# Decay attention and two MLPs on one core: the last tile's scores of two heads by one block-diagonal matrix of queries, and a new order

## The chip, the cores and the metric

The kernel runs on one core of a Trainium2 chip. The metric is device microseconds of one execution. Five engines run side by side, each through its own instructions in a fixed order: TensorE (PE in the profile, with its weight loads as PEld), VectorE (DVE), ScalarE (ACT), GpSimd (POOL) and the queue that issues the transfers (SP). They wait for each other on semaphores.

## The reference, cut to what matters

```python
# q, k, v: (4 batches, 8 heads, 576 positions, 64 dims); f: (4, 8, 576)
scores = q @ k.T / 8
cum = np.cumsum(np.log(np.clip(f, 0.0001, 1.0)), axis=-1)
scores = np.where(causal, -1e9, scores + cum[..., :, None] - cum[..., None, :])
scores = scores - scores.max(-1, keepdims=True)
attn = np.exp(scores)
attn = attn / (attn.sum(-1, keepdims=True) + 1e-9)
x = (attn @ v)                      # reshaped to (2304 tokens, 512)
x = relu(x @ moe_w_in) ** 2 @ moe_w_out          # 512 -> 2048 -> 512
g = x @ moe2_w_gate                              # 512 -> 1536
out = (silu(g) * (x @ moe2_w_val)) @ moe2_w_out  # 1536 -> 512
```

All inputs and the output are float32.

## The kernel before, in words

**Precision.** TensorE multiplies float16 or rounded float32. A float32 operand is split into a high and a low part and three products (high by high, high by low, low by high) are added up in PSUM. The passes (0,0), (0,1), (1,0) in the code are these three.

**Attention.** A unit is one batch and two heads: 16 units. Both heads' queries and keys lie in one tile, dims by positions, head 0 on partitions 0 to 63 and head 1 on 64 to 127, so a product over one head's 64 dims uses half of the array's rows. Query positions are cut in tiles of 128. The first 256 (two tiles) of all units are the early half, the positions 256 to 575 the late half: two tiles of 128 queries and a last tile of 64, called the tail, which the late half takes first. For the tail the 576 keys are cut in two pieces of 288 (`cuts`), and the code makes one step of six products for each piece: three passes by two heads, each of 64 contraction rows (line 802, `scores`). Head 0 has 64 columns of queries. Head 1 takes 128 columns (the last 128 queries), so that its 64 wanted rows come out on PSUM partitions 64 to 127; the other 64 rows are not read. Each head has its own PSUM tile.

After the scores: VectorE adds the decay and finds the minimum (line 825), ScalarE takes the exponential (845) and the high part of the probabilities (904), VectorE the low part (908), a DMA transposes them, TensorE multiplies by the values (955, `mix`), ScalarE and VectorE keep the result as `x` (978, 983). On the way in, ScalarE rounds keys and queries (742, 735), GpSimd takes their low parts (745, 738) and masks the decay table (786).

**MLPs.** Tiles of 256 tokens. The first MLP's first product is line 1151 into `h`; ScalarE applies relu, square and the cast (1173, 1180, 1194), GpSimd the low part (1199), and line 1221 is its second product into `acc`, which ScalarE and VectorE empty at the end of a tile (1240, 1242). The second MLP is lines 1417 and 1533. Weights arrive as float32, are looked through for a scale (407, 324, 333) and split in two float16 parts on ScalarE and VectorE (378, 381, 386, 466, 470).

**The order.** Nothing is scheduled at run time. `Plan` collects steps with an engine, an assumed duration, what they depend on and which buffers they take; its `order()` walks through them once and gives each engine, when it is free, the ready step with the lowest number in `pri`. The tables `EPRI`, `VPRI`, `IPRI`, `ILOAD`, `OPRI`, `OLOAD` and `GPRI` hold such numbers for the early attention units and for the loading of weights; `FREE` says how many of the four pieces of the first weight matrix load without waiting for the first decay table. The result is a written-out list for each engine, which the engines run through in that order, whether or not the assumed durations were right.

**Fillers.** `keep_clock` (line 293) is a product of ones into a spare PSUM bank, 130 times, of the lowest priority: the plan puts one where TensorE would have nothing and a bank of `h` is free. All 130 stand in TensorE's list and are carried out, wherever they came to stand.

Of the kernel before, what the change touches and what calls it, by code (L numbers as in the profile page):

```python
# [9 lines left out]
F32R = mybir.dt.float32r  # L10
# [4 lines left out]
AF = mybir.ActivationFunctionType  # L15
# [3 lines left out]
PE, ACT, DVE, POOL, SP = "PE", "ACT", "DVE", "POOL", "SP"  # L19
AFTER = {PE: 0.25, ACT: 0.2, DVE: 0.15, POOL: 0.2, SP: 0.0, None: 0.0}  # L20
DMA_ISSUE = 0.45
QUEUE = 8
PORT = {DVE: 1.0, POOL: 0.45}
GLO = 9
SUMV = 3
# [31 lines left out]
class Plan:  # L57
# [104 lines left out]
    return 0.1 + n * 0.0021  # L162


GPRI = 863
GATE0 = -1
GATE = 5
EPRI = [97, 98, -1473, -437, 74, 58, -88, -342, 192, 243, 591, 593, 223, 341, 56, -118]
VPRI = [79, -116, 547, 595]
IPRI, ILOAD = [573, -458, 265, 171], [-574, -104, -303, 434]  # L170
OPRI, OLOAD = [157, 400, 363, 178], [-547, 34, 61, 213]
VERBOSE = False
WHOLE = 2
SQUARE = 7
FREE = 4
COPY = (ACT, ACT)
ROUNDS = [(0, 1), (8,), (2, 3), (4, 5), (6, 7)]
LAST = ROUNDS[-1]
# [3 lines left out]
def decay_attention_moe_kernel(ctx: ExitStack, tc, q, k, v, f, w1, w2, wg, wv, wo, outT):  # L182
    nc = tc.nc
    P = 128
    B, H, _, S = q.shape
# [7 lines left out]
    TAIL = S // P  # L193
    NB = TAIL + 1
    SPLIT = 256
    QW = S - SPLIT
# [6 lines left out]
    AN, ACC = 4, 2  # L203
# [16 lines left out]
    ps_at = attn_ctx.enter_context(tc.tile_pool(name="ps_at", bufs=AN, space=bass.MemoryType.PSUM))  # L220
    pools = {}
# [7 lines left out]
    add = plan.add  # L229
# [13 lines left out]
    one = table("one", 1)  # L243
# [13 lines left out]
    def prev(tag):  # L257
        return alloc_chain.get(tag)
# [296 lines left out]
    XFIRST, XSTAT = {}, {}  # L555
# [117 lines left out]

            XSTAT["x8"] = add(DVE, 0.7, widest, [XSTAT[x] for x in range(B)], pri)

    SCALED, BIAS = {}, {}

    def attn_unit(idx, b, pr, half, opened):
        early = half == 0
        whole = early and b < WHOLE  # L680
        pri = EPRI[idx] if early else 10 * idx
# [6 lines left out]
        q0 = 0 if early else SPLIT  # L688
# [4 lines left out]
        c = {}  # L693
# [55 lines left out]
        KA, QA = (kr, qr) if early else (kq_buf("KA"), kq_buf("Q"))  # L749
# [15 lines left out]
        VT = vu["buf"]  # L765
        seen = {0: [], 1: []}
        for ti, i in enumerate(tiles):
# [24 lines left out]
            mm = None  # L792
            for ci, (n0, n1) in enumerate(cuts):

                def scores(heads=heads, n0=n0, n1=n1, ti=ti, ci=ci):
                    for h in range(2):
                        c["ps", ti, ci, h] = at_tile()
                    for qi, ki in ((0, 0),) if early else ((0, 0), (0, 1), (1, 0)):
                        for h, _, _, qc, M, _ in heads:
                            rows = slice(64 * h, 64 * h + 64)  # L800
                            Q, K = (c["qr"], c["kr"]) if early else (c["Q"][:, qi], c["K"][:, ki])
                            nc.tensor.matmul(  # L802
                                c["ps", ti, ci, h][:M, : n1 - n0], Q[rows, qc - q0 : qc - q0 + M],
                                K[rows, n0:n1], start=(qi, ki) == (0, 0), stop=early or qi == 1,
                            )

                bufs = [*sbufs, cg_buf] if ci == 0 else []
                pbufs = [Buf("ps_at", AN) for _ in range(2)]
                mm = add(PE, (4 if early else 3) * (0.06 + (n1 - n0) * 0.00048), scores, [*ready, opened], pri,
                         take=[*pbufs, *bufs], order=[mm, *(prev(x.tag) for x in bufs)])  # L810
# [128 lines left out]
            def mix(st=st, i=i, nb=nb, w=w, ti=ti):  # L939
                c["av", ti] = ps = at_tile()  # L940
                for blk in range(nb if whole else 0):
                    for h in range(2):
                        nc.tensor.matmul(
                            ps[64 * h : 64 * h + 64, :w], vu["vr"][:, blk, 64 * h : 64 * h + 64], st["PT"][:, h, blk, :],
                            start=blk == 0, stop=blk == nb - 1,
                        )
                for blk in range(nb if not whole else 0):
                    K = min(P, S - blk * P)
                    for a, va in ((0, 0), (0, 1), (1, 0)):
                        for h in range(2):  # L950
                            if i == TAIL:
                                rhs = st["PT"][:K, 0, a, blk, 64 * h : 64 * h + 64]
                            else:
                                rhs = st["PT"][:K, h, a, blk, :]
                            nc.tensor.matmul(  # L955
                                ps[64 * h : 64 * h + 64, :w], vu["VT"][:K, blk, h, va, :], rhs,
                                start=(blk == 0 and (a, va) == (0, 0)), stop=(blk == nb - 1 and a == 1),
                            )

            o = P * i - q0  # L960
# [4 lines left out]
            mx = add(PE, 0.05 + nb * 0.3 if whole else 0.2 + nb * 6 * 0.03, mix, [tn, *vu["in"], XSTAT[xk], opened], pri,  # L965
                     take=[pbuf])
            t_buf.users.append(mx)
            VT.users.append(mx)

            kx = XS[:, b : b + 1] if whole else kx_of(xk, b, pr)  # L970
# [634 lines left out]
    def open_half():  # L1605
        h0_ctx.close()
        pools["at"] = attn_ctx.enter_context(
            tc.tile_pool(name="at", bufs=1, side="right", reuse_waits="tile")
        )

    opened = fence(open_half, half0_ops)
    for b in range(B):
# [116 lines left out]
```

## Time and profile before

| | us |
|---|---|
| median of 3 runs (lowest, highest) | 956.33 (955.98, 957.39) |
| the profiled execution's own time | 958.73 |
| its span, first to last instruction | 957.0 |
| TensorE busy with products | 945.6 |
| VectorE busy | 621.3 |
| ScalarE busy | 603.4 |
| GpSimd busy | 315.2 |

Busy times are unions: two products of which one starts before the other ends count once. The duration of one product is from its start to its modelled end and includes the way through the array, so products that follow each other closely overlap; what a product adds to the time is the distance from its start to the next one's start.

### The profile page before, as it was taken

To read this page: it belongs to the slowest core of one execution; us is meant where nothing else is said; L and a number is where in the kernel's file an instruction comes from. 1 tells how busy PE (TensorE), PEld (TensorE's weight loads), DVE (VectorE), ACT (ScalarE), POOL (GpSimd) and SP (SyncE) were. 2 spreads that over 40 slices of the span, in tenths; PEclk is the share of its full clock that TensorE was granted. 3 is DMA by queue.
4 is the path that set the end of the run, shared out by engine and by line. 5 is a ranking of instruction groups with operands and counts; after the bars stand their busy time and mean duration, and the time that the engine had idled before them with its cause. 6 is when DMAs were issued, how large, how long until landed. Compare 5 with 4: busy or idle time off the path is not lost.

```text
span 957.0 us, 22589 instructions
## 1 busy us (share of the span) xinstructions
PE 945.6 (99%) x8941; PEld 735.7 (77%) x8941; DVE 621.3 (65%) x1438; ACT 603.4 (63%) x1145; POOL 315.2 (33%) x422
## 2 busy tenths in 40 slices
PE   8999999999999999999999999999999999999998
PEld 4578777887777877778888887778977776877774
DVE  5689878576766788787989897445464363433331
ACT  5899898697788897777978675235343343332332
POOL 1332054354444353443335453031311241111120
PEclk9999999999999999999999999999999999999999
DMA  8796339687968799999934411002020001000101
GB/s 285 231 340 215 97 78 225 187 212 143 192 147 186 183 229 182 252 242 243 206 110 177 155 48 42 1 2 89 2 67 1 1 2 45 2 1 12 34 1 45
DMA packets 147946, 117.48 MB, mean 123 GB/s; under 512 B 98240, under 2 KB 136128, under 8 KB 142592
## 3 DMA queue, kind: packets, MB, share of 16 engines
q1 hardware_dynamic: 147840, 116.04, 46.7%
q8 instruction: 70, 1.15, 0.5%
q14 instruction: 36, 0.29, 0.1%
HBM read 83.44 MB, written 9.51 MB: 97 GB/s over the span
## 4 chain that ended last, share of the span: by engine, by line
PE 54%; DVE 1%; ACT 0%; issue 0%; DMA 0%; SPq 0%; DVEq 0%; ACTq 0%
PE v L1417 15%; PE acc L1533 14%; PE h L1417 11%; PE acc L1221 7%; PE h L1151 6%; PE ps L955 1%; PE ps L802 1%; DVE ms L1287 0%; DVE p L908 0%; DVE s L825 0%; DMA out_dram<-tmp 0%; DVE sq L1291 0%; SPq L1591 0%; DVE VT L630 0%; DVE tmp L1564 0%
## 5 line engine op out<-in xcount | busy, mean ns | idle before, releaser
L1151 PE MATMUL h<-x,i 128*128 128x256 f16 x1728 | 208.4, 273 | 0.7 <-ACT hold L1173 0.7
L1221 PE MATMUL acc<-g,o 128*128 128x256 f16 x1728 | 208.0, 273 | 0.0
L1151 PEld LDWEIGHTS <-i 128*128 128x128 f16 x1728 | 163.0, 98 | 29.3 <-issue 8.4
L1221 PEld LDWEIGHTS <-o 128*128 128x128 f16 x1728 | 163.8, 98 | 27.4 <-issue 6.0
L1533 PE MATMUL acc<-o,f 128*128 128x512 f16 (+1 forms) x720 | 145.9, 358 | 0.9 <-ACT o L1506 0.5
L1533 PEld LDWEIGHTS <-f 128*128 128x128 f16 x720 | 70.0, 98 | 65.0 <-issue 1.4
L1199 POOL TENSOR_TENSOR g<-tmp,g 128x512 f16<-128x512 f32 x56 | 76.1, 1360 | 130.7 <-ACT g L1194 126.0
L1496 POOL TENSOR_TENSOR tmp<-tmp,o 128x256 f32<-128x256 f32 (+1 forms) x30 | 23.5, 784 | 247.7 <-ACT o L1490 247.3
L786 POOL TENSOR_SCALAR_AFFINE_SELECT bias<-bias 128x128 f32<-128x128 f32 (+1 forms) x160 | 60.9, 390 | 106.3 <-DVE cg L825 58.3
L908 DVE SCALAR_TENSOR_TENSOR p<-s,cg,p 128x512 f16<-128x512 f32 (+4 forms) x112 | 76.0, 695 | 24.9 <-ACT p L904 24.4
L845 ACT ACTIVATE s<-s,cg 128x256 f32<-128x256 f32 (+4 forms) x144 | 83.0, 578 | 13.8 <-DVE cg L825 13.5
L825 DVE CUSTOM_DVE_ANT_0 s<-ps,bias 128x512 f32<-128x512 f32 (+3 forms) x160 | 72.6, 481 | 29.4 <-PE ps L802 21.4
L904 ACT ACTIVATE p<-s,cg 128x512 f16<-128x512 f32 (+4 forms) x112 | 67.1, 615 | 9.5 <-DVE cg L858 4.6
L1462 ACT ACTIVATE r<-r,ms 128x768 f32<-128x768 f32 (+1 forms) x30 | 26.1, 871 | 74.1 <-DVE r L1434 74.0
L1417 PEld LDWEIGHTS <-g 128*128 128x128 f16 x720 | 65.4, 98 | 8.5 <-issue 0.6
L1417 PEld LDWEIGHTS <-v 128*128 128x128 f16 x720 | 65.4, 98 | 6.5
L1417 PE MATMUL v<-i,g 128*128 128x256 f16 (+1 forms) x540 | 67.9, 262 | 0.2 <-DVE tmp L1434 0.2
L1417 PE MATMUL v<-i,v 128*128 128x256 f16 (+1 forms) x540 | 67.9, 262 | 0.0
L1434 DVE TENSOR_TENSOR r<-r,h 128x512 f32<-128x512 f32 (+1 forms) x30 | 19.0, 633 | 73.7 <-PE h L1417 65.1
L1434 DVE TENSOR_TENSOR r<-r,v 128x512 f32<-128x512 f32 (+1 forms) x60 | 38.1, 634 | 33.8 <-PE v L1417 31.7
L1500 POOL TENSOR_TENSOR r<-r,o 128x768 f32<-128x768 f32 (+1 forms) x30 | 45.4, 1513 | 39.6 <-ACT o L1493 38.7
L1417 PEld LDWEIGHTS <-eg 128*128 128x128 f16 x540 | 49.3, 98 | 8.9
(186 smaller groups left out, 1604.2 us busy)
## 6 DMA issues: line engine op xcount, KB each, us to landing
raw<-in_moe_w_out_dram SPq DMA_DIRECT2D x11, 1024.0 KB, 6.5
bias<-cum_d SPq DMA_DIRECT2D x16, 576.0 KB, 4.8
raw<-in_moe_w_val_dram SPq DMA_DIRECT2D x9, 1024.0 KB, 5.7
raw<-in_moe_w_gate_dram SPq DMA_DIRECT2D x9, 1024.0 KB, 6.7
raw<-in_moe_w_in_dram SPq DMA_DIRECT2D x8, 1024.0 KB, 7.1
vr<-in_v_dram SPq DMA_DIRECT2D x32, 256.0 KB, 4.2
x_d<-tmp SPq DMA_DIRECT2D x18, 256.0 KB, 2.7
kr<-in_k_dram SPq DMA_DIRECT2D x16, 288.0 KB, 4.2
```

What stands on the lines that cost most here:

```text
L786: nc.gpsimd.affine_select(diag, diag, pattern=[[-1, w]], compare_op=ALU.is_ge, fill=-8e9, base=0, channel_multiplier=1)
L825: nc.vector.tensor_tensor_reduce(out=s[r0:r1, n0:e1], in0=c["ps", ti, ci, h][r0:r1, : e1 - n0], in1=c["bias"][r0:r1, h, n0:e1], scale=-0.1 ...
L845: nc.scalar.activation(s[:, :ext], s[:, :ext], AF.Exp, bias=cg[:, mc : mc + 1], scale=-1.0, accum_out=cg[:, 2:3],)
L904: nc.scalar.activation(pv[:, 0, :ext], s[:, :ext], AF.Copy, scale=cg[:, 3:4])
L908: nc.vector.scalar_tensor_tensor(pv[:, 1, :ext], s[:, :ext], cg[:, 3:4], pv[:, 0, :ext], op0=ALU.mult, op1=ALU.subtract,)
L1151: nc.tensor.matmul(HP[key][:, u, :], w[:, wi, kk, c * P : (c + 1) * P], x[:, xi, kk, :], start=(kk == 0 and (wi, xi) == (0, 0)), stop=(kk ...
L1199: lows[2].tensor_tensor(G[k0][1][:, 1], G[k0][0], G[k0][1][:, 0], op=ALU.subtract)
L1221: nc.tensor.matmul(acc[:, d - part[0], :], w[:, wi, c, d * P : (d + 1) * P], G[k0][1][:, gi, u, :], start=(m == 0 and d == part[0] and (wi ...
L1417: nc.tensor.matmul(R[reg][:, which, :w], t[:, wh, w1_ : w1_ + P], x[:, xh, xi, kk], start=fresh and which == 0 and kk == 0 and (wh, xh) == ...
L1434: nc.vector.tensor_tensor(out(), x(), y(), op=ALU.add)
L1500: nc.gpsimd.tensor_tensor(g, g, R["g"][:, 0, 1:4], op=ALU.subtract)
L1533: nc.tensor.matmul(acc_of(d), wd[:, cc, d * P : (d + 1) * P], R["g"][:, gi, 2 * m : 2 * m + 2].rearrange("p a t -> p (a t)"), start=mm == ...
```

## The change: what it does

The tail's two heads now share their products. A new tile `both` (two buffers, taken in turn by even and odd units) holds for the high and for the low part of the queries a matrix of 128 by 128: head 0's 64 tail queries in the upper left quarter, head 1's in the lower right, zeros elsewhere. The zeros are written once, by two ScalarE instructions where the late half opens; two GpSimd copies for each unit bring in the queries. With this matrix as the stationary operand one product over all 128 rows gives head 0's scores on PSUM partitions 0 to 63 and head 1's on 64 to 127 of one bank. So a unit's tail needs six products (three passes by two pieces of keys) of 128 rows, 128 columns and 288 keys, in place of twelve of 64 rows, and they stand in one step, both pieces together, in place of two steps. VectorE's and all later instructions keep their forms.

Beside that: the numbers of the priority tables and `FREE` (4 to 2) are others, the plan's assumed durations for late scores and for `mix` are others, and `mix` is rewritten for groups of tiles, which `MERGE = (0, 0)` leaves switched off (one tile a group, as before).

```diff
+TAIL_US = 0.95
+MERGE = (0, 0)
-GPRI = 863
+GPRI = 842
-EPRI = [97, 98, -1473, -437, 74, 58, -88, -342, 192, 243, 591, 593, 223, 341, 56, -118]
+EPRI = [370, 281, -956, -100, 16, 121, -583, -685, 358, 313, 446, 543, -150, 12, -61, -51]
...
-FREE = 4
+FREE = 2
...
+            both = Buf("both%d" % (idx % 2), 1)
+            def corner(h):
+                def copy():
+                    r = slice(64 * h, 64 * h + 64)
+                    nc.gpsimd.tensor_copy(BOTH[idx % 2][r, :, r], c["Q"][r, :, QW - 64 : QW])
+                return copy
+            b0 = take(POOL, 0.3, corner(0), [qh, ql], [both], use=[QA])
+            b1 = add(POOL, 0.3, corner(1), [qh, ql], pri, use=[QA, both], order=[b0])
+            tail_ready = [kh, kl, b0, b1]
...
-                heads = [(0, 0, 64, S - 64, 64, 0), (1, 64, 128, S - 128, 128, 0)]
+                heads = [(0, 0, 64, S - 64, 64, 0), (1, 64, 128, S - 64, 64, 0)]
...
+                def tail_scores(cuts=cuts, ti=ti):
+                    for cc, (m0, m1) in enumerate(cuts):
+                        c["ps", ti, cc, 0] = c["ps", ti, cc, 1] = at_tile()
+                        for qi, ki in ((0, 0), (0, 1), (1, 0)):
+                            nc.tensor.matmul(
+                                c["ps", ti, cc, 0][:, : m1 - m0], BOTH[idx % 2][:, qi], c["K"][:, ki, m0:m1],
+                                start=(qi, ki) == (0, 0), stop=qi == 1,
+                            )
...
+                if i == TAIL:
+                    if ci == 0:
+                        tbufs = [Buf("ps_at", AN) for _ in cuts]
+                        mm = add(PE, TAIL_US, tail_scores, [*tail_ready, opened], pri, take=[*tbufs, *bufs],
+                                 use=[both], order=[prev(x.tag) for x in bufs])
+                    pbufs = [tbufs[ci]] * 2
...
+        for n in range(2):
+            BOTH[n] = pools["at"].tile([P, 2, P], F32R, tag=f"both{n}", name="both")
+            nc.scalar.activation(
+                BOTH[n].rearrange("p a q -> p (a q)"), one[:, 0:1].to_broadcast([P, 2 * P]), AF.Copy, scale=0.0
+            )
```

In the changed kernel the lines have other numbers: 293 is 295, 1151 is 1193, 1221 is 1263, 955 is 995, 802 is 817 and, for the tail, 826; GpSimd's 738 is 740, 786 is 801, and the copies are 767.

What this makes of the order, first on TensorE at the first tail. `KA` is the keys, `Q` and `both` the queries, `i` and `o` weights of the first MLP. Before:

```order
L1221 MATMUL acc<-g,o_1320 128x256
L802 MATMUL ps<-KA,Q 64x288
L802 MATMUL ps<-KA,Q 128x288
L802 MATMUL ps<-KA,Q 64x288
L802 MATMUL ps<-KA,Q 128x288
L802 MATMUL ps<-KA,Q 64x288
```

and so on to twelve. Now:

```order
L1193 LDWEIGHTS i_614
L1193 MATMUL h<-x,i_614 128x256
L826 MATMUL ps<-KA,both 128x288 x6
L817 MATMUL ps<-KA,Q 128x512 x6
L1193 LDWEIGHTS i_614
```

The twelve half-row products are six of 128 rows. Over the whole list there were 29 visits to line 802 for tails (26 of six products and 3 of twelve) and are 16 visits to line 826 of six.

Second, on TensorE, the fillers around the first product of line 1221. Before, 15 of them stand there, the last of the 130:

```order
L1151 LDWEIGHTS i_1374
L1151 MATMUL h<-x,i_1374 128x256
L293 LDWEIGHTS ones
L293 MATMUL ps<-ones 128x512
L293 LDWEIGHTS ones
L293 MATMUL ps<-ones 128x512
```

Now one stands there:

```order
L1193 LDWEIGHTS i_1302
L1193 MATMUL h<-x,i_1302 128x256
L295 LDWEIGHTS ones
L295 MATMUL ps<-ones 128x512
L1263 LDWEIGHTS o_1219
L1263 MATMUL acc<-g,o_1219 128x256
```

and 19 stand late in the attention, around the tail of a unit near the end:

```order
L295 LDWEIGHTS ones
L295 MATMUL ps<-ones 128x512
L817 MATMUL ps<-KA,Q 128x384 x6
L826 MATMUL ps<-KA,both 128x288 x6
L295 LDWEIGHTS ones
L295 MATMUL ps<-ones 128x512
```

Ahead of the first product of line 1221 there were 130 fillers and are 109; two more come after the 19.

Third, on GpSimd, where the third late unit's queries are split. Before:

```order
L745 TENSOR_TENSOR KA<-kr,KA 128x576
L738 TENSOR_TENSOR Q<-qr,Q 128x320
L921 MEMSET p_3489 128x2x64
L1199 TENSOR_TENSOR g<-tmp,g 128x512
L786 AFFINE_SELECT bias<-bias 128x128 x2
```

Now:

```order
L747 TENSOR_TENSOR KA<-kr,KA 128x576
L801 AFFINE_SELECT bias<-bias 128x128
L740 TENSOR_TENSOR Q<-qr,Q 128x320
L801 AFFINE_SELECT bias<-bias 128x128
L767 COPY both<-Q 64x2x64 x2
L1241 TENSOR_TENSOR g<-tmp,g 128x512
```

The two copies of the unit stand behind the low part of its queries and ahead of a low part of the MLP.

## Rows read from the trace of the kernel before

**Rows 1.** The page: busy time by engine.
```profile
PE 945.6 (99%) x8941; PEld 735.7 (77%) x8941; DVE 621.3 (65%) x1438; ACT 603.4 (63%) x1145; POOL 315.2 (33%) x422
```

**Rows 2.** The chain that ended last, by engine.
```profile
PE 54%; DVE 1%; ACT 0%; issue 0%; DMA 0%; SPq 0%; DVEq 0%; ACTq 0%
```

**Rows 3.** Waits of PE, 0 to 480 us: us in total, times, longest.
```profile
PE ps L407 <- DVE raw L386: 1.1, 2, 0.6
PE ps L802 <- DVE cg L825: 0.9, 1, 0.9
```

**Rows 4.** Timeline of PE: start, length, products (three parts of it).
```profile
185.55 2.13 PE L1221 MATMUL acc<-g,o 128*128 128x256 f16 x18
187.61 1.06 PE L802 MATMUL ps<-KA,Q 64*64 64x288 f32 x12
...
188.60 1.49 PE L1151 MATMUL h<-x,i 128*128 128x256 f16 x12
...
198.94 0.83 PE L1221 MATMUL acc<-g,o 128*128 128x256 f16 x6
199.70 0.66 PE L802 MATMUL ps<-KA,Q 64*64 64x288 f32 x6
200.29 0.83 PE L1221 MATMUL acc<-g,o 128*128 128x256 f16 x6
```

**Rows 5.** Groups by line and form: busy, mean ns, idle before.
```profile
L802 PE MATMUL ps<-KA,Q 64*128 64x288 f32 x96 | 20.1, 320 | 0.0
...
L879 PEld LDWEIGHTS ps<-p,s 128*128 128x128 f32 x96 | 11.5, 191 | 1.3 <-issue 1.0
```

**Rows 6.** Timeline of PE at line 879, float32 over all 128 rows.
```profile
49.62 1.69 PE L293 MATMUL ps<-ones 128*128 128x512 bf16 x7
51.15 1.50 PE L879 MATMUL ps<-p,s 128*128 128x128 f32 x12
```

**Rows 7.** Timeline of PE at the first product of line 1221.
```profile
117.92 3.83 PE L293 MATMUL ps<-ones 128*128 128x512 bf16 x15
121.60 1.67 PE L1221 MATMUL acc<-g,o 128*128 128x256 f16 x13
```

**Rows 8.** Stretches: us, busy of PE, PEld, DVE, ACT, POOL, clock, DMA share, GB/s.
```profile
60.00:147.00 87.00, 86.23 (x790) 69.62 (x788) 74.65 (x220) 79.65 (x167) 27.08 (x50) 1.00 0.53 155
147.00:190.00 43.00, 42.96 (x453) 34.55 (x449) 29.73 (x98) 33.10 (x82) 16.99 (x27) 1.00 0.85 203
190.00:300.00 110.00, 110.00 (x1269) 87.90 (x1268) 75.13 (x202) 89.12 (x184) 51.45 (x84) 1.00 0.80 175
...
400.00:480.00 80.00, 79.62 (x945) 63.40 (x944) 66.00 (x171) 63.58 (x125) 29.97 (x44) 1.00 0.98 229
```

**Rows 9.** Waits of ACT, 60 to 150 us.
```profile
ACT hold L1173 <- PE h L1151: 4.2, 8, 1.9
ACT g L1194 <- PE acc L1221: 1.9, 3, 1.1
```

**Rows 10.** Timeline of ACT, what two products of line 1221 wait for.
```profile
119.84 1.12 ACT L1194 CAST g<-hold 128x512 f16<-128x512 f32 x2
...
146.24 0.67 ACT L1240 ACTIVATE tmp<-acc,fy 128x512 f32<-128x512 f32 x1
```

**Rows 11.** Timeline of PE at the second of these.
```profile
147.34 0.82 PE L1221 MATMUL acc<-g,o 128*128 128x256 f16 x6
```

**Rows 12.** Groups of POOL by form: busy, mean ns, idle before.
```profile
L738 POOL TENSOR_TENSOR Q<-qr,Q 128x320 fp32r<-128x320 f32 x16 | 14.6, 912 | 2.9 <-ACT Q L735 2.9
...
L786 POOL TENSOR_SCALAR_AFFINE_SELECT bias<-bias 64x64 f32<-64x64 f32 x32 | 10.0, 312 | 6.7 <-DMA bias<-cum_d 5.5
...
L635 POOL MEMSET vr<- 64x128 f32 x32 | 6.1, 202 | 19.3 <-PE ps L943 7.2 <-issue 6.2 <-DVE cg L855 2.6
```

**Rows 13.** Timeline of POOL, low part of the first late unit's queries.
```profile
185.56 0.87 POOL L738 TENSOR_TENSOR Q<-qr,Q 128x320 fp32r<-128x320 f32 x1
```

**Rows 14.** Groups of ACT by form, the nearest to the new zeroing.
```profile
L904 ACT ACTIVATE p<-s,cg 128x512 f16<-128x512 f32 x32 | 22.6, 715 | 0.3 <-ACT g L1194 0.3
```

More of the change, by code (lines that the diff above doesn't have):

```diff
@@ L162, in pool_us @@
     return 0.1 + n * 0.0021
-GPRI = 863
+GPRI = 842
 GATE0 = -1
 GATE = 5
-EPRI = [97, 98, -1473, -437, 74, 58, -88, -342, 192, 243, 591, 593, 223, 341, 56, -118]
-VPRI = [79, -116, 547, 595]
-IPRI, ILOAD = [573, -458, 265, 171], [-574, -104, -303, 434]
-OPRI, OLOAD = [157, 400, 363, 178], [-547, 34, 61, 213]
+EPRI = [370, 281, -956, -100, 16, 121, -583, -685, 358, 313, 446, 543, -150, 12, -61, -51]
+VPRI = [320, -45, 495, 593]
+IPRI, ILOAD = [594, 50, 424, 193], [-390, 134, 653, 441]
+OPRI, OLOAD = [129, 425, 371, 295], [-993, 530, -621, 354]
 VERBOSE = False
@@ L674, in v_batch @@
             XSTAT["x8"] = add(DVE, 0.7, widest, [XSTAT[x] for x in range(B)], pri)
-    SCALED, BIAS = {}, {}
+    SCALED, BIAS, BOTH = {}, {}, {}
     def attn_unit(idx, b, pr, half, opened):
@@ L766, in attn_unit @@
         seen = {0: [], 1: []}
+        done_tiles = []
         for ti, i in enumerate(tiles):
@@ L805, in scores @@
                             )
-                bufs = [*sbufs, cg_buf] if ci == 0 else []
-                pbufs = [Buf("ps_at", AN) for _ in range(2)]
-                mm = add(PE, (4 if early else 3) * (0.06 + (n1 - n0) * 0.00048), scores, [*ready, opened], pri,
-                         take=[*pbufs, *bufs], order=[mm, *(prev(x.tag) for x in bufs)])
+                def tail_scores(cuts=cuts, ti=ti):
[6 more added lines that the diff above has]
+                            )
+                bufs = [*sbufs, cg_buf] if ci == 0 else []
+                if i == TAIL:
[4 more added lines that the diff above has]
+                    pbufs = [tbufs[ci]] * 2
+                else:
+                    pbufs = [Buf("ps_at", AN) for _ in range(2)]
+                    mm = add(PE, (4 if early else 3) * (0.06 + (n1 - n0) * 0.00048) + (0 if early else 0.12), scores, [*ready, opened], pri,
+                             take=[*pbufs, *bufs], order=[mm, *(prev(x.tag) for x in bufs)])
                 for x in bufs:
@@ L936, in attn_unit @@
                 tn = take(SP, 1.4, turn, lows, [t_buf], use=[p_buf], nbytes=TURN_COST * n_turn * 32768, late=TURN_LATE)
-            def mix(st=st, i=i, nb=nb, w=w, ti=ti):
-                c["av", ti] = ps = at_tile()
[L941 to L949, printed above, removed]
+            done_tiles.append((i, nb, w, st, tn, t_buf))
@@ L950, in mix @@
+            if i != TAIL and len(done_tiles) < 2 and MERGE[half]:
+                continue
+            group, done_tiles = done_tiles, []
+            lo_tile = min(g[0] for g in group)
+            w = sum(g[2] for g in group)
+            def mix(group=group, lo_tile=lo_tile, ti=ti):
+                c["av", ti] = ps = at_tile()
+                for i, nb, w, st, _, _ in group:
+                    at = P * (i - lo_tile)
+                    for blk in range(nb if whole else 0):
                         for h in range(2):
[L951 to L954, printed above, removed]
@@ L955, in mix @@
                             nc.tensor.matmul(
-                                ps[64 * h : 64 * h + 64, :w], vu["VT"][:K, blk, h, va, :], rhs,
-                                start=(blk == 0 and (a, va) == (0, 0)), stop=(blk == nb - 1 and a == 1),
-                            )
-            o = P * i - q0
+                                ps[64 * h : 64 * h + 64, at : at + w], vu["vr"][:, blk, 64 * h : 64 * h + 64],
+                                st["PT"][:, h, blk, :], start=blk == 0, stop=blk == nb - 1,
+                            )
@@ new lines, in mix @@
+                    for blk in range(nb if not whole else 0):
+                        K = min(P, S - blk * P)
+                        for a, va in ((0, 0), (0, 1), (1, 0)):
+                            for h in range(2):
+                                if i == TAIL:
+                                    rhs = st["PT"][:K, 0, a, blk, 64 * h : 64 * h + 64]
+                                else:
+                                    rhs = st["PT"][:K, h, a, blk, :]
+                                nc.tensor.matmul(
+                                    ps[64 * h : 64 * h + 64, at : at + w], vu["VT"][:K, blk, h, va, :], rhs,
+                                    start=(blk == 0 and (a, va) == (0, 0)), stop=(blk == nb - 1 and a == 1),
+                                )
@@ L961, in attn_unit @@
+            o = P * lo_tile - q0
             xk, xo = ("x8", 64 * b) if i == TAIL else (b if early else B + b, o)
@@ L964, in attn_unit @@
             pbuf = Buf("ps_at", AN)
-            mx = add(PE, 0.05 + nb * 0.3 if whole else 0.2 + nb * 6 * 0.03, mix, [tn, *vu["in"], XSTAT[xk], opened], pri,
+            us = sum(nb * 0.3 if whole else 0.8 - 0.2 if i == TAIL else nb * 6 * 0.028 for i, nb, *_ in group)
+            mx = add(PE, 0.05 + us if whole else 0.2 + us, mix, [*(g[4] for g in group), *vu["in"], XSTAT[xk], opened], pri,
                      take=[pbuf])
-            t_buf.users.append(mx)
+            for g in group:
+                g[5].users.append(mx)
             VT.users.append(mx)
@@ L1609, in open_half @@
         )
+        for n in range(2):
+            BOTH[n] = pools["at"].tile([P, 2, P], F32R, tag=f"both{n}", name="both")
+            nc.scalar.activation(
+                BOTH[n].rearrange("p a q -> p (a q)"), one[:, 0:1].to_broadcast([P, 2 * P]), AF.Copy, scale=0.0
+            )
     opened = fence(open_half, half0_ops)
```

## The prediction

> **What bounds the kernel now.** I read the page's busy times first: TensorE has a product in flight in 945.6 of 957.0 us, the next engine in 621.3 [rows 1]. The chain that ended last says the same by another way, PE 54% against 1% for VectorE and nothing for the others [rows 2]. Busy is not proof, since 130 fillers count in it, so I went to the waits of PE: in the first 480 us, which hold all of attention, the two longest sums are 1.1 and 0.9 us [rows 3]. TensorE therefore runs through its list almost without a stop, and the time is the sum of what stands in that list. The reader should see two things here. A product taken out of the list is worth its distance to the next start, not its duration. And an instruction that is hidden today is hidden behind a TensorE that is never early; if TensorE gets ahead, others may come to be waited for.
>
> **What the tail costs before.** Six products of 288 keys begin at 199.70 and the next block at 200.29: 0.59 us. The six products of 256 before them begin at 198.94, 0.76 us ahead, though such products stand 0.109 apart (18 in the 2.06 us from 185.55 to 187.61, with the same extra in them, or 6 x 0.109 = 0.65): entering the half-row block costs another 0.09 to 0.1. The block of twelve takes 0.99 [rows 4]. So a visit of six costs about 0.69 and one of twelve 1.09. With 26 and 3 visits: 26 x 0.69 + 3 x 1.09 = 21.2. Four visits follow a block that is itself half an array and pay less on entry; read one by one the 29 come to 18.2 inside and 2.5 on entry, 20.7 us.
>
> It matters that the twelve are not twelve times 288 columns. From a visit of six to one of twelve the cost grows by 0.40 for six products, so two heads' products already run side by side, 0.13 for a pair; 192 durations of 320 ns [rows 5] would be 61 us and mislead. The change halves the number of instructions, but not the columns that stream through: six times 288 in either form. What it can save is the ends of each visit, the second visit of a unit, and the little by which a pair is dearer than one product.
>
> **What it costs after.** No row shows a rounded float32 product over all 128 rows with 288 columns. From below: 15 products of 512 and a wait take 3.68 us (117.92 to 121.60) [rows 7], seven of them 1.53 us, 0.216 each [rows 6], so columns cost 0.42 ns and 288 of them 0.122; six make 0.73 and 16 units 11.8 us. The stationary load must fit under that: line 879 loads 128 rows of float32 for each of 12 products that stand 0.111 apart at its steady part (1.43 us in all, with the switch to the next block) [rows 6], though one load is recorded with 191 ns [rows 5]; loads overlap, and 0.111 is under 0.122. Nor is there an entry cost: seven fillers ahead of line 879 take 7 x 0.216 and 0.02 more, though the type changes there from bfloat16 to float32. From above: a first load that is not hidden, 0.08 a visit, 13.1 us; and far above, two passes for each product as line 879's plain float32 has them, 6 x 0.245 x 16 = 23.5. I take 11.8, the end that line 879's row is nearest to in what matters, the missing entry. Saved: 20.7 - 11.8 = 8.9.
>
> On what hides a load there is a rule against this change: the Trainium skill, "TensorE: Matmul & The Clock Gate", Part 3, The mechanism, says that a weight load overlaps a running matmul only when the row group differs, which full-array products give up. By it each product would pay its load too, 6 x (0.122 + 0.107) a visit, with the same page's 128 columns / 1.2 GHz (LDWEIGHTS), an estimate, 22.0 us for 16, more than before. The trace speaks against it: full-array products with a load each stand 0.109 apart in rows 4.
>
> **The rest of TensorE's list.** I added the measured distance of every pair of neighbouring forms along both lists: 944.7 us before and 936.6 after, 8.1 less. That is the 8.9 less 0.8, since the new order switches between full and partial blocks ten times more often elsewhere (308 against 298 without the tails). The fillers are 130 in both.
>
> **Other engines.** GpSimd gets 32 copies of 64 partitions by 128 elements, a form the trace lacks. From below 0.202 (a memset of 64 by 128), from above 0.912 (the split of 128 by 320); I take 0.312, the mask of 64 by 64 [rows 12]: 10 us over the stretch in which GpSimd is idle for more than half (51.45 of 110 busy) [rows 8]. Behind them stand masks and low parts of the MLP. The first unit has the least room: its queries are split at 186.43 [rows 13] and its tail begins at 187.61 [rows 4], 1.2 us, which two copies of 0.312 fit into. ScalarE's two zeroings are under 0.715 each [rows 14], in a stretch where it is busy 33.1 of 43 us [rows 8]. No transfer is added; VectorE keeps its instructions. All these I cost at nothing.
>
> **What is late next.** With 21 fillers fewer ahead of it (4.5 us) and other moves, TensorE's list reaches the first product of line 1221 6.2 us earlier. Its input comes from ScalarE's casts, which end at 120.96, 0.6 us ahead of the product at 121.60 [rows 7, 10]; later ScalarE empties a bank of `acc` until 146.91, 0.4 us ahead of the product at 147.34 that writes it anew [rows 10, 11]. So there is little room: ScalarE, busy 79.65 of 87 us [rows 8], must come 6 us earlier too. Of its 7.4 us of idleness there 4.2 + 1.9 are waits for TensorE [rows 9], which shrink when TensorE is earlier. At best nothing is lost, at worst 6.2 us. I take 2.5, a bit less than half, because most of the idleness is of the kind that goes. The 19 fillers near the end of attention do not buy this back: they run whether or not TensorE is late there.
>
> Sum, against the profiled execution: 957.0 - 8.1 + 2.5 = 951.4 of span, and 1.7 outside it, 953.1. The profiled execution is 2.4 above the median of the runs, so for the median 956.33 - 5.6 = **950.7 us**.
>
> **Rivals.** The measurement of this kernel can tell about 0.2%, 1.9 us, from no change: faster is under 954.4, slower above 958.2.
> - *Nothing is lost.* ScalarE follows entirely: 956.3 - 8.1 = 948.2. For it: its waits are for TensorE. Against: the 0.4 to 0.6 us of room at two products. 0.20.
> - *ScalarE sets the front.* All 6.2 us come back as standing time: 954.4. For it: VectorE, which feeds ScalarE's exponentials and splits, is itself busy 74.65 of 87. Against: nearly all of ScalarE's idleness there is TensorE's. 0.15.
> - *The fillers turn against it (slower).* TensorE stands still in the front for ScalarE, and the 19 postponed fillers (4.1 us) then run on top of a TensorE that is late, and whose attention inputs are ready. Price 6.2 + 4.1 = 10.3, time 958.5; it decides from 8.1 us of new standing time on. For it: transfers fill 0.98 of 400 to 480 us [rows 8], so that stretch can't be shortened at will either. Against: PE hardly waits in any stretch today. 0.07.
> - *The full-array product is dearer (slower).* Loads in series, 10.2 us more: 960.9, the rule above; two passes: 962.4. Against: rows 4 and 6. 0.05.
> - *The change of type, not of rows, makes the entry.* Then entry and exit, 0.19 a visit, remain and 3 us less is saved: 953.7. Against: no entry cost at line 879. 0.05.
>
> **How the numbers follow.** The forecast has 0.48, its own range 949 to 953. Faster: forecast, nothing lost, the type rival, and about a third of the front rival, 0.78. Slower: the two marked so, mostly, 0.10, which also leaves room for an order that stalls at a place I have not seen. Within: 0.12. The range reaches from 0.8 under the best case, 947.4, to 957.4.
>
> **What would show it.** Right: TensorE busy or not, six products of line 826 begin and the next block stands 0.73 to 0.8 us later, with no 0.09 on entry; some 12 us for 16 visits; waits of PE between 60 and 150 us that sum to 1 to 4 us, on ScalarE's casts or relu; the rest of attention shifted by about 5 us; the second MLP's stretch as long as before. Wrong: visits of 1.3 us or more (products in series or in two passes); a wait of line 826 for GpSimd; standing time over 8 us before 480 us, on whatever engine.

## The result and the profile after

The changed kernel is slower: median 961.50 us (958.61 to 964.03, 6 runs) against 956.33, ratio 1.0054 with a 95% interval of 1.0035 to 1.0072. Its profiled execution took 961.26 us, span 959.5.

The page of the changed kernel, busy time and the chain that ended last, answering to [rows 1, 2]:

```profile
PE 942.1 (98%) x8845; PEld 737.9 (77%) x8845; DVE 625.8 (65%) x1438; ACT 604.2 (63%) x1147; POOL 329.5 (34%) x454
...
PE 91%; DMA 3%; DVE 2%; ACT 1%; issue 1%; SPq 1%; POOL 0%; DVEq 0%; ACTq 0%; POOLq 0%
```

TensorE is busy 3.5 us less in a span that is 2.5 us longer: it stands still 6 us more. Where, the waits of PE in the first 480 us tell (us in total, times, longest), answering to [rows 3]:

```profile
PE acc L1263 <- POOL g L1241: 2.7, 3, 1.0
PE ps L409 <- DVE raw L388: 2.2, 3, 1.3
PE ps L817 <- DMA qr<-in_q_dram: 1.8, 1, 1.8
PE ps L295 <- DVE pw L305: 1.2, 1, 1.2
```

The first of these lies where the prediction looked: three waits, at 122, 149 and 169 us, for low parts of the MLP that GpSimd makes behind ScalarE's casts. A wait of 0.7 us for such a cast itself, at 168 us, comes on top. None of them is due to the copies into `both`, of which the first runs at 190.6 us.

The tail did become shorter. The timeline of PE at two tails, answering to [rows 4]:

```profile
202.89 0.80 PE L817 MATMUL ps<-KA,Q 64*128 64x384 f32 x6
203.62 1.06 PE L826 MATMUL ps<-KA,both 128*128 128x288 f32 x6
204.52 2.79 PE L1193 MATMUL h<-x,i 128*128 128x256 f16 x24
...
223.10 1.48 PE L1263 MATMUL acc<-g,o 128*128 128x256 f16 x12
224.34 1.03 PE L826 MATMUL ps<-KA,both 128*128 128x288 f32 x6
225.21 1.48 PE L1193 MATMUL h<-x,i 128*128 128x256 f16 x12
```

From 223.10 to 225.21 are 2.11 us; twelve products of 256 at 0.109 are 1.31 of it, so the visit costs 0.80, for both pieces of keys. Where half-row scores stand ahead it takes 0.90 inside and some 0.1 on entry. Ten of the 16 visits are of the first kind, six of the second: about 14.0 us, not the 11.8 of the sum.

The loss begins in the front. PE from 54 to 73 us:

```profile
53.81 0.83 PE L1193 MATMUL h<-x,i 128*128 128x256 f16 x6
...
56.63 1.12 PE L409 MATMUL ps<-raw 128*128 128x128 bf16 x8 [1.34 <-DVE raw L388]
...
60.59 1.65 PE L817 MATMUL ps<-kr,qr 64*128 64x256 f32 x8 [1.77 <-DMA qr<-in_q_dram]
62.18 2.74 PE L1193 MATMUL h<-x,i 128*128 128x256 f16 x12
...
72.73 0.16 PE L335 MATMUL ps<-top,ones 2*128 2x1 bf16 x1 [0.66 <-DVE top L332]
```

And two stretches of it (busy of PE, PEld, DVE, ACT, POOL, then clock, DMA share, GB/s), to be held against 10.00 and 9.35 of PE at a clock of 1.00 in the same stretches of before:

```profile
50.00:60.00 10.00, 7.24 (x52) 4.81 (x50) 7.60 (x28) 9.53 (x21) 2.32 (x4) 0.99 0.98 369
60.00:70.00 10.00, 9.41 (x56) 7.17 (x57) 8.17 (x24) 7.53 (x16) 4.28 (x8) 0.67 0.77 294
```

The reader should see three things: TensorE comes to the first MLP product at 53.81, 5.9 us earlier than in the profiled execution of before (59.71), and then waits for a weight whose two halves VectorE joins (line 388) and for a query transfer, with one filler in all (at 54.47); in the last of these waits the granted clock falls to half, so that twelve products take 2.74 us from 62.18, in [rows 4] 1.49; and ScalarE, 9.53 busy in the first stretch, is 7.53 in the second.

Of the 5.9 us, 2.6 are not the order's: the profiled execution of before had a wait of 0.9 us and then half the clock from 31.3 to 34.7 us, and the same list in the kernel called "block in old order" below, without them, comes to that product at 57.06. The stretch in both, that of before first:

```profile
30.00:40.00 10.00, 9.40 (x43) 4.60 (x44) 7.24 (x35) 8.80 (x23) 4.81 (x13) 0.83 0.87 283
30.00:40.00 10.00, 10.00 (x62) 5.75 (x60) 8.56 (x30) 8.68 (x23) 3.78 (x9) 1.00 0.87 295
```

Starts of the nth product of the first MLP's first layer, read from the traces, for the kernels of the experiments as well:

```
n                      1     49    337   1009   1105   1201   1441
before               59.7   68.8  112.5  361.5  393.1  425.3  494.1
after                53.8   72.8  115.7  358.7  389.3  428.8  496.6
block in old order   57.1   66.4  110.0  354.4  385.6  417.1  485.5
new front            54.0   73.0  115.9  360.8  392.1  423.7  492.0
old front            59.1   68.9  112.6  358.1  388.9  429.6  496.9
new order whole      54.4   73.3  116.2  357.6  388.8  427.1  494.9
fillers in waits     53.8   72.1  117.1  358.1  389.8  432.2  499.9
```

Each row is one execution. Before, block in old order and old front have the same list in the front; that they differ there by 2.0 to 2.6 us is the clock, as said above.

### The profile page after: what moved, and what is told of

Same layout as the page of the kernel before. It is cut to its first block, busy times and chain, and to the rows that moved or that the text cites. A ratio compares the mean times of both kernels' runs of the same rounds, so it can differ in the third digit from the quotient of the medians.

```text
span 959.5 us, 22448 instructions
## 1 busy us (share of the span) xinstructions
PE 942.1 (98%) x8845; PEld 737.9 (77%) x8845; DVE 625.8 (65%) x1438; ACT 604.2 (63%) x1147; POOL 329.5 (34%) x454
## 4 chain that ended last, share of the span: by engine, by line
PE 91%; DMA 3%; DVE 2%; ACT 1%; issue 1%; SPq 1%; POOL 0%; DVEq 0%; ACTq 0%; POOLq 0%
PE h L1193 20%; PE acc L1263 18%; PE acc L1575 14%; PE v L1459 14%; PE h L1459 10%; PE ps L995 4%; PE ps L817 4%; PE ps L295 3%; PE ps L826 1%; PE ps L910 1%; DMA qr<-in_q_dram 1%; DMA raw<-in_moe_w_out_dram 1%; DMA raw<-in_moe_w_in_dram 1%; PE ps L983 1%; DMA bias<-cum_d 1%
## 5 line engine op out<-in xcount | busy, mean ns | idle before, releaser
L1241 POOL TENSOR_TENSOR g<-tmp,g 128x512 f16<-128x512 f32 x56 | 72.4, 1292 | 121.3 <-ACT g L1236 114.9
L801 POOL TENSOR_SCALAR_AFFINE_SELECT bias<-bias 128x128 f32<-128x128 f32 (+1 forms) x160 | 63.4, 405 | 93.2 <-DMA bias<-cum_d 46.9
L939 DVE SCALAR_TENSOR_TENSOR p<-s,cg,p 128x512 f16<-128x512 f32 (+4 forms) x112 | 79.1, 726 | 20.7 <-ACT p L935 20.0
```

The costliest lines, as they stand in the source:

```text
L801: nc.gpsimd.affine_select(diag, diag, pattern=[[-1, w]], compare_op=ALU.is_ge, fill=-8e9, base=0, channel_multiplier=1)
L939: nc.vector.scalar_tensor_tensor(pv[:, 1, :ext], s[:, :ext], cg[:, 3:4], pv[:, 0, :ext], op0=ALU.mult, op1=ALU.subtract,)
L1241: lows[2].tensor_tensor(G[k0][1][:, 1], G[k0][0], G[k0][1][:, 0], op=ALU.subtract)
```

## The experiments

Theory A: the block-diagonal tail saves what its visits show, and the new order costs more than that in standing time. Rival B: the block-diagonal step itself (its copies, its one step of two tiles) makes TensorE stand. Of before, 11 to 24 runs on the same chips gave medians of 957.4 to 957.9. Ratios are to these; differences between kernels are given between medians, and by the ratios they would be up to 1.5 us larger or smaller.

**The new step and the new numbers apart.** Three ways: the changed kernel with the old numbers (its assumed durations stay), the old kernel with the new numbers, and the old kernel with only the tail's products replaced, every step at its old place.

```diff
-GPRI = 842
+GPRI = 863
...
-FREE = 2
+FREE = 4
```

> The changed kernel with the number tables of the kernel before (GPRI, EPRI, VPRI, IPRI, ILOAD, OPRI, OLOAD, and FREE 4): the block-diagonal tail in nearly the old order. Theory A (the tail itself saves about 7.8 us, the new numbers cost about 11 to 13 us of standing time, most of it at 54 to 76 us): 948 to 950 us, TensorE's waits of the front back to those of before. Rival B (the block-diagonal step itself makes TensorE stand, by its GpSimd copies and the one step that holds two tiles): 958 to 962 us. Rival C (both by halves): 952 to 956.

Measured: 973.52 us, ratio 1.0167 (1.0153 to 1.0181). The second has the same lines with the signs turned, in the old kernel:

> The kernel before with the new number tables and FREE 2, half-row tails kept. Theory A: the standing time without the saving, 966 to 969 us, the stretch 54 to 76 us as in the changed kernel. Rival B: 955 to 957, as before. Rival C: 959 to 963.

Measured: 979.92, 1.0232 (1.0214 to 1.0249). Both miss every theory: from the same numbers with the other graph of steps the planner makes a third order, worse than either. The number tables can't be tested without their graph. So the order has to be held fixed:

```diff
+                def tail_scores(n0=n0, n1=n1, ti=ti, ci=ci):
+                    c["ps", ti, ci, 0] = c["ps", ti, ci, 1] = at_tile()
+                    for qi, ki in ((0, 0), (0, 1), (1, 0)):
+                        nc.tensor.matmul(
+                            c["ps", ti, ci, 0][:, : n1 - n0], BOTH[idx % 2][:, qi], c["K"][:, ki, n0:n1],
+                            start=(qi, ki) == (0, 0), stop=qi == 1,
+                        )
...
+            for h in range(2):
+                r = slice(64 * h, 64 * h + 64)
+                nc.gpsimd.tensor_copy(BOTH[idx % 2][r, :, r], c["Q"][r, :, QW - 64 : QW])
```

> The kernel before with its order kept instruction for instruction, and the tail's products alone replaced: at each of the two old places of a unit's tail three full-array products by the block-diagonal queries, the copies within the GpSimd step of the low query parts. Theory A: 956.3 less 7 to 8 us, 948.5 to 950 us. Rival B: 956 or above. If the full-array product is what costs, the visits of three take over 0.5 us each.

Measured: **950.97** (949.89 to 952.32), 0.9936 (0.9924 to 0.9948): 6.4 us faster than before, 10.5 faster than the changed kernel's median, and the best of all kernels run, though 1 us above the range of theory A. Its waits of PE in the first 480 us (in this kernel and those made from it the tail is line 801, other scores 813, the first MLP's layers 1162 and 1232):

```profile
PE ps L407 <- DVE raw L386: 1.4, 2, 0.8
PE ps L293 <- POOL ones L277: 1.1, 1, 1.1
PE h L1162 <- ACT hold L1184: 0.9, 1, 0.9
```

Two of its visits of three products:

```profile
196.00 0.83 PE L1232 MATMUL acc<-g,o 128*128 128x256 f16 x6
196.58 0.64 PE L801 MATMUL ps<-KA,both 128*128 128x288 f32 x3
197.07 0.83 PE L1232 MATMUL acc<-g,o 128*128 128x256 f16 x6
```

From 196.00 to 197.07 less 0.65 are 0.42 (0.41 by the unrounded starts), where the half-row visit of six cost 0.70 [rows 4]. Rival B falls: the step pays, copies and all.

**The order alone.** The same instructions in the changed kernel's order: the list that the planner returns is replaced by one written out.

```diff
-    order = plan.order()
+    order = [plan.steps[n] for n in ORDER]
```

> The kernel of 951.0 us with all steps in the changed kernel's order, so that beside it only the order differs, all instructions being the same. Theory A2: 961 to 962.5 us, the changed kernel's time. If the separate GpSimd copies or the one visit of six products cost something by themselves: under 959.

Measured: 961.42 (959.53 to 965.60), 1.0042 (1.0025 to 1.0059): the changed kernel's time again, 10.5 us above the old order with the same instructions. On every engine but GpSimd, where only the copies stand in other places, the instructions come in the changed kernel's order. So the order is the cause, and the separate copies and the joined visit cost nothing that shows.

**Front and rest apart.** The same edit with other lists; both orders have nearly the same steps ahead of the first product of line 1232, which is where they were cut.

> The other half: the front up to the first product of MLP 1's second layer in the changed kernel's order, the rest in the old order, the block-diagonal tail as in the run of 951.0 us; the 21 fillers that the new front doesn't hold are left out. Theory A2: 956 to 957.5 us, with the waits at 55 to 73 us and half clock near 60 us as in the changed kernel, and none near 400 us. Rival (the rest of the old order takes the front's loss back, because ScalarE and VectorE bound it): 951 to 953.

Measured: 956.84 (955.73 to 959.66), 0.9987 (0.9976 to 0.9997), 5.9 above the old order whole, as theory A2 had it. In the table of starts it stands 6.6 behind at n = 49 and 6.5 at 1441: nothing of the front's loss is given back.

> The kernel of the run with the block-diagonal tail in the old order (951.0 us), with every engine's steps from the first product of MLP 1's second layer (the line that the changed kernel has as L1263, near 120 us) on in the changed kernel's order; the front keeps the old order, with all 130 fillers in it. Theory A2 (two separate losses: 5.6 us in the new order of the front, by milestones of the two traces, and 5 to 6 us in the new order at 395 to 480 us): 956 to 957.5 us, the loss of the late stretch alone. Rival (the late loss is only the front's, pushed on): 951 to 952. Rival (the late loss follows from a TensorE that comes early, so it grows when the front is faster): 959 to 962.

Measured: 959.69 (956.33 to 962.18), 1.0015 (1.0000 to 1.0030), 8.7 above the old order whole. That median lies between two groups: six executions took 956.3 to 958.8, at a mean granted clock of 0.995 to 1.000, and six 960.6 to 962.2, at 0.994 to 0.996. The first group agrees with theory A2, the second with the rival by which the late loss grows when the front is faster. The profiled execution is of the second. It loses 2.5 us by n = 49, where the list is the old one and the clock was 0.83 from 20 to 30 us, and most of the rest between n = 1105 and 1201 (3.3 behind, then 12.5). PE there:

```profile
412.64 0.66 PE L801 MATMUL ps<-KA,both 128*128 128x288 f32 x3 [0.20 <-DVE x L994]
417.10 1.17 PE L966 MATMUL ps<-PT,VT 128*64 128x128 f16 x18 [3.80 <-DVE cg L836]
...
421.01 1.69 PE L1162 MATMUL h<-x,i 128*128 128x256 f16 x14 [0.51 <-DVE x L994]
```

5.9 and 8.7 are more than 10.5. That the two losses overlap, as a list that is late in front would wait less behind, is not shown: by the ratios the excess is 0.0024, with an interval of some 0.0028 to either side, worked out from those of the four kernels in it.

**The late fillers.** The changed kernel without the last 21:

```diff
+            if st.fn is keep_clock and begun:
+                continue
+            begun = begun or st.fn is not None and "mlp_pair" in st.fn.__qualname__ and st.fn.__name__ == "go2"
```

> The changed kernel without the 21 fillers (products whose result nobody reads, which hold the clock) that its order puts behind the first 100 us. Theory A, in which these run on a TensorE that has work: 957 to 959.5 us, 2 to 4.5 us under the changed kernel (21 by 0.2135 is 4.5). If they only fill waits: no change, 961 to 962. If the clock falls where they are taken out: above 962, with a stretch at half clock near 400 us.

Measured: 962.22 (958.88 to 963.65), 1.0046: no change that the intervals can tell. In the profiled execution the 4.5 us come back as waits (PE of this kernel):

```profile
413.25 0.67 PE L826 MATMUL ps<-KA,both 128*128 128x288 f32 x3 [1.35 <-DVE x L1025]
416.81 1.17 PE L995 MATMUL ps<-PT,VT 128*64 128x128 f16 x18 [2.89 <-DVE cg L856]
```

And the clock falls to half there, from 413.9 to 420.7 us, the third of the cases expected. The stretch in this kernel, then in the changed one:

```profile
400.00:420.00 20.00, 15.76 (x173) 12.28 (x172) 14.41 (x45) 11.36 (x25) 7.33 (x15) 0.85 1.17 202
400.00:420.00 20.00, 18.70 (x196) 13.33 (x194) 16.31 (x49) 12.37 (x26) 7.99 (x17) 1.00 1.15 243
```

So the fillers fill a wait that is there without them, and hold the clock in it. Two of the six executions, at a mean granted clock of 0.996, took 958.9 and 959.2, the four at 0.990 to 0.993 962.1 to 963.7: whether the fillers cost some 2 us where the clock holds without them, six executions leave open.

**The half clock in the front.** Products on ones put where TensorE waits:

```diff
+PAD = {486: 8, 527: 9}
...
+                    warm_up(c["ps", ti, ci, 0], PAD.get(at_step["step"], 0))
```

> The kernel of the run before in this list (new order whole), with 17 products on ones added where TensorE waits in the front: 8 ahead of the transposes before the second Gram product of an output weight, 9 ahead of the scores that wait for the query transfer. If the half clock near 60 us is part of the front's price (6.6 us at half clock in the changed kernel, some 3 us): 2 to 3 us under the run without them, with no stretch at half clock there. If the waits alone are the price: within 0.7 us of it. If the added products push TensorE's own work back: 1 to 3.6 us above it (17 by 0.2135 is 3.6).

Measured: 964.33 (961.63 to 965.80), 1.0063, 2.9 above the order without them. The clock did stay up; the three stretches of this kernel:

```profile
50.00:60.00 10.00, 8.79 (x60) 5.67 (x59) 7.60 (x28) 8.23 (x20) 2.33 (x4) 1.00 1.02 363
60.00:70.00 10.00, 10.00 (x77) 6.95 (x76) 8.99 (x31) 9.61 (x19) 5.22 (x11) 1.00 0.82 312
70.00:80.00 10.00, 8.57 (x70) 6.38 (x68) 7.37 (x26) 8.05 (x20) 2.49 (x9) 0.83 0.60 145
```

The fall of the clock comes 10 us later and is half as long, 3.4 us for 6.8. By the size this is the third case expected, by the place it is not: in the table of starts this execution is 1.2 us ahead of the new order whole at n = 49, 1.0 and 0.5 behind it at 337 and 1009, and 4.1 of the 5.7 us by which it ends later come between 1105 and 1201, where its clock was at half from 417.1 to 420.5 and the other's was not. So in the front the added products, 3.7 us of them, about pay for themselves, and no time is won; what the half clock costs there this run does not settle. Of the changed kernel's six runs, three at a mean granted clock of 0.998 took 958.6 to 961.7 and three at 0.995 took 961.3 to 964.0, which speaks for some 2 us.

**Fifteen fillers fewer in the old order.** Whether ScalarE sets the first product of line 1232:

> The kernel of 951.0 us without the last 15 of its 130 fillers, which stand at 115 to 119 us, ahead of the first product of MLP 1's second layer. If ScalarE's work, not TensorE's, sets the time of that product: 950 to 952 us, no change, TensorE waiting some 3 us there. If TensorE's own list sets it: 15 by 0.2135 is 3.2 us less, 947.5 to 948.5. If the clock falls in the gap: 951 to 954.

Measured: 953.77 (952.50 to 957.93), 0.9960 (0.9948 to 0.9972), 2.8 above the kernel with them, the intervals just touching. PE and the stretch after it, in a profiled execution that took 957.93, the longest of the eleven:

```profile
121.07 0.27 PE L1232 MATMUL acc<-g,o 128*128 128x256 f16 x1 [2.41 <-ACT g L1205]
```

```profile
120.00:130.00 10.00, 7.91 (x56) 6.32 (x56) 4.71 (x13) 8.41 (x15) 3.98 (x5) 0.83 0.00 0
```

ScalarE does set it: of 3.2 us of fillers 2.4 come back as a wait, and the clock falls right behind it, to 0.83 over 120 to 130 us (1.00 with them). Here the fillers earn their place, as far as touching intervals tell.

**Which steps of the order.** Four local repairs, and two of them together. The queries' transfer earlier, ahead of the value loads:

> The run with the new front and the old late order (956.8 us), with one pair of SyncE's loads, the key and query transfer that TensorE waits for near 60 us, issued as early as in the old order, ahead of the value loads. If the late transfer is the front's price (1.4 to 1.8 us of wait, and the 2.4 us that ScalarE stands behind it): 953 to 955 us, TensorE's wait for the transfer gone. If the weights, now later by the same 0.3 MB, are late in its place: 956 to 958.

Measured: 955.66 (953.69 to 957.02), 0.9979 (0.9970 to 0.9988). The wait for the transfer fell from 1.4 to 0.5, the time by 1.2 us, between the two cases expected and with intervals that overlap: if it is part of the price, it is not most of it. With the weights ahead of the value loads too:

> The run with the new front, the old rest and the queries asked for early (955.7 us), with the steps of the second batch's last three value tiles (their loads, maxima and scale) put back by 27 steps on all engines, so that the weight loads go ahead of most value loads, as in the old order. If the order of the loads is what the front costs: 951.5 to 954 us, and the waits for joined weights (2.7 us) under 1.5. If it is the order on ScalarE and VectorE: 955 to 956.5.

Measured: 961.66 (959.35 to 963.23), 1.0038: 6.0 worse and outside both cases: TensorE's longest wait in the front is now 4.2 us for a maximum (line 333), the waits for joined weights are still 1.8, and the clock was at half from 56.8 to 67.0 us. In the late stretch, first the looks at MLP 2's weights put back to their old neighbours:

> The run with the old front and the new late order (959.7 us), with one group of steps put back to its old places: the first looks at MLP 2's value and gate weights (a 1 MB load each, a maximum on VectorE, and the scale from it), which the new order asks for one load earlier, ahead of two DMA transposes of attention weights. If these loads make the transposes late and TensorE stand at 417 us (3.8 us there, SyncE held 10.1 us by two transposes behind such a load): 3.5 to 8 us less, 952 to 956 us, no wait over 1 us at 400 to 425. If VectorE or ScalarE is late there for another reason: 958.5 to 960.5.

Measured: 983.55, 1.0280: 24 us worse, with waits of 5.4 and 4.7 us, the first for the looks' own maxima. Whether the looks are needed where the new order has them, or the steps that follow them lost their places, the run doesn't tell, so it decides nothing. Then only the last two, all engines alike:

> The run with the old front and the new late order (959.7 us), with the last two of the four looks at MLP 2's weights (their loads, maxima and scales) put back by 52 of some 4,000 steps on all engines alike, so that the 1 MB load asked for at 402.9 us comes behind the two transposes instead of ahead of them; nothing else changes its turn until 470 us. If that load holds up the transposes and they TensorE: its wait of 3.8 us near 417 us goes, 954 to 957 us. If TensorE waits there for another reason: 959 to 961. If the looks are needed sooner than that, as in the run before: above 962.

Measured: 965.18 (963.43 to 965.95), 1.0069, 5.5 worse, in the third case. But the wait that it was meant for did shrink. SyncE's queue in the run with the old front, and then in this one:

```profile
402.88 0.36 SPq L1047 DMA_DIRECT2D raw<-in_moe_w_val_dram  x1
...
404.42 10.14 SPq L943 DMA_TRANSPOSE PT<-p  x2
```

```profile
402.59 6.58 SPq L943 DMA_TRANSPOSE PT<-p  x2
409.23 0.69 SPq L1047 DMA_DIRECT2D raw<-in_moe_w_val_dram  x1
```

PE in the latter:

```profile
412.69 1.17 PE L966 MATMUL ps<-PT,VT 128*64 128x128 f16 x18 [1.69 <-DVE cg L836]
...
452.50 0.66 PE L801 MATMUL ps<-KA,both 128*128 128x288 f32 x3 [3.51 <-DVE x L994]
```

With the 1 MB load behind them the two transposes take SyncE 6.58 us in place of 10.14, and TensorE waits 1.69 in place of 3.80 and 4.4 us earlier; 40 us on it waits 3.51 for something else, with the clock at half from 453.6 to 457.0. That the load was what held the transposes is not shown. In the changed kernel it stands ahead of them just so, and they take 6.62 us:

```profile
404.42 0.36 SPq L1078 DMA_DIRECT2D raw<-in_moe_w_val_dram  x1
...
405.93 6.62 SPq L963 DMA_TRANSPOSE PT<-p  x2
```

Both repairs in the whole new order:

> The run with the whole new order (961.4 us), with the two small edits together: the key and query transfer asked for early, the last two looks 52 steps later; the late fillers left out. If the two waits are its price: 955 to 958 us. If each edit only hands the time to the next wait: 960 to 963.

Measured: 967.74 (965.50 to 973.43), 1.0105, 6.3 above that order unmended, which had its late fillers: no time is won, TensorE's longest wait is now 3.6 us for `x` (line 994), and the clock was at half from 453.6 to 460.5 us.

## Why the prediction was wrong

- **The tail: right in mechanism, too large.** 8.9 was the term, 8.1 with the rest of the list; 6.4 (5.0 to 7.3) is what the replacement alone brought. The term of 11.8 was too small in two ways. Its price of a column came from bfloat16 fillers, 0.122 for 288 columns; a visit behind full-array products costs 0.80, which is 0.133 a product, as a half-row pair cost before [rows 4]. And an entry cost stays where half-row scores stand ahead, six times of 16. The 13.1 that I named as an upper bound for a first load that isn't hidden was nearer to the 14.0 than the value I took, but not by its reason: a visit of three costs 0.41 and one of six 0.80, so the first product costs no more than the others. That loads go in series, as the Trainium skill, "TensorE: Matmul & The Clock Gate", Part 3, The mechanism, would have it for full-array products, the trace denies: by the prediction's estimate from that page a visit would take 1.37 us, and it takes 0.80 to 1.0.
- **The other engines: right.** No wait of line 826 for GpSimd stands among PE's waits; the copies (0.29 us each in the trace, where I took 0.312) and the zeroings (0.405 each) cost nothing that shows: 6.4 us are saved with both of them in.
- **What is late next: this step failed.** I took 2.5 us of new standing time, at worst 6.2; the order alone costs 10.5. The working looked at one place, the first product of line 1221, took TensorE's lead there as the whole price, and asked whether ScalarE could follow. At that place it was about right: from 122 to 169 us TensorE waits 3.4 us for ScalarE's casts and the low parts made from them. But most of the front's loss lies 50 us ahead of it, at 54 to 73 us, where the new list brings TensorE 3.3 us earlier than the old one (57.1) to inputs that aren't there yet (a weight's join, a query transfer), with a single filler left between 54 and 73 us where before had nine; by n = 49 it is 6.5 us behind that kernel. At the first product of line 1221 the changed kernel was at 121.1 us, before at 121.6 and the block in old order at 119.2: the lead of 6.2 had become 0.5, or 2.0 us of lag. The second place, at 400 to 425 us, I named only for its fillers: I took them for 4.1 us of a TensorE that has work there. In the profiled execution without them the same time passes in waits and at half the clock.
- **The rivals.** "ScalarE sets the front" holds of the old order, by the run with 15 fillers fewer; of what the new order loses it is the 3.4 us above, a part only. "The fillers turn against it" had the sign, but 958.5 is 2.2 us above before where 5.2 were measured, and its mechanism is not borne out: without the late fillers no time is won. The chance of 0.10 for slower also left "room for an order that stalls at a place I have not seen", which is what came; it had no price.
- **The bound that was missing.** A new order has as many places to stall as it has waits. The trace of before bounds it only from below (nothing lost); the worst case that I gave was that of one place.
- **Still open:** which steps of the new order cost the 10.5 us. Front and rest are apart by runs (5.9, and 6 to 10 in two groups), and the query transfer accounts for at most some 1.2 of the front, within the noise. What makes TensorE wait near 417 us, and how much of the front is waits and how much half clock, was only read from traces, not shown; no repair brought the late time back.

## What to carry to other kernels

When a change comes with a new order, run the new instruction at its old place first: here that one run gave 0.9936, and with the run of the order alone it showed that the order had spent the gain and more. Numbers that steer a planner belong to their graph of steps; with the other graph they made orders 1.7 and 2.3% slower here. A wait that a trace shows is not yet time to be won: of five local repairs one brought at most 1.2 us, and four cost 5.5 to 24 us. And a trace is one execution: compare its front with a second execution of the same list before a lead or a lag is put down to the order.

## What the hardware showed unasked

- Rounded float32 products over all 128 rows, each with its own load of 128 columns (recorded with 186 to 192 ns), start 0.126 to 0.141 us apart at 288 columns, 0.46 ns a column; the bfloat16 fillers of 512 columns start 0.216 apart, 0.42. The first of a visit starts 0.03 us behind a float16 product in place of 0.109, and the second 0.22 behind the first, which together is what two ordinary steps take.
- Two DMA transposes held SyncE 10.14 us behind a 1 MB load in one execution, 6.62 behind it in another kernel's, and 6.58 ahead of it in a third. What stands behind them in the queue waits as long.
- In the changed kernel the granted clock fell to half (1.2 GHz) at 59.7 us, in the third of three waits of TensorE (1.34, 0.24 and 1.77 us), and stayed there until 66.6, though TensorE was busy again from 60.6. Fillers put into the waits kept it up until 72.3, and won no time.
